# DFT odd sums added in the even sums' bank, with the low half and the doubled even sum taken out by ScalarE, and the patterns redrawn

## The chip, the cores and the metric

The kernel runs on one core of a Trainium2 chip. The metric is the device time of one execution in microseconds. The profile names the engines PE (TensorE, matmuls; PEld is its weight load), ACT (ScalarE), DVE (VectorE), POOL (GpSimd) and SP (SyncE, which only issues DMAs here). PE writes its results into eight banks of PSUM; ACT and DVE take them out from there.

## What is computed

```
X   = real(fft(fft(x, axis=1), axis=2))        # x: 8 x 3008 x 256, float32
h   = max(X.reshape(24064, 256) @ w_in, 0)     # w_in: 256 x 2048
out = (h * h) @ w_out                          # w_out: 2048 x 256
```

A Fourier transform over 3008 rows and 256 features, of which the real part is kept, and then a feed-forward layer with a squared ReLU.

## The kernel before

**Stage 1, the DFT over rows.** For each of the eight batches, DVE folds x into symmetric and antisymmetric parts (`fold_ops`, L353 to L390: operations on tiles u, v and w). PE multiplies w with cosine and sine tables (`cosT`, `sinT`). The sum over six row groups q is split into even and odd q (`par` 0 and 1), since the result at row k is even + odd and the result at the mirrored row is even - odd or odd - even. So two sums of some 377 columns give 754 columns of the tiles `pt` (cosine part, sn 0) and `qt` (sine part, sn 1). This is done for two blocks of columns (`blk` 0 and 1), so that each batch has four such pairs of sums; the batches in `INL`, 0 and 1, add six matmuls per `qt` pair for an extra row (`ez`), the others get that row from `e_ops`, for three batches at a time. `dft_ops` (L400) makes the list of pieces: a piece is three matmuls. In the kernel before, each sum has a PSUM bank of its own, the tile `pf`. When the even sum is complete ACT copies it to the tile `as` (L418); when the odd sum is complete DVE writes the low half (L453, or L449 with a sign) and the high half (L455, L457 or L450), each from `as` and the odd sum's bank. Batch 0's first block is done by `stage1_first` (L466).

**Stage 2, the first layer.** The feature transform is folded into w_in: `gmat` (L323) makes G1 and G2, `gneg` (L334) makes G3 = -2 G2 on all rows but the last. Columns of pt and qt go through in 25 chunks, two of 256 columns, then 512 each, the last of 264. A chunk that crosses the end of a batch has two segments, and each of its matmuls is split. A chunk has 16 units of 128 hidden features. A unit first makes G1 pt + G2 qt in a bank `xb`, takes out its ReLU, and then needs the same for the mirrored row. The kind of the unit, a letter in `KINDS`, says how the mirrored row is made:

- r: a third matmul with G3 into the same bank, and a second ReLU on ACT (L738)
- v: the third matmul too, and the ReLU on DVE (L735)
- d: no third matmul; DVE takes -2 xb + edge out between the two matmuls (L716), and adds it to xb afterwards (L727)
- q: as d, but ACT takes the first part out (L713) and POOL adds the edge (L714)
- p: as d, with the edge made by POOL (L694) and not by DVE (L697)

`x_front` and `x_take` start a unit, `x_back` ends it two steps later. `x_square` squares the results, two units at a time: on DVE (L750), or where `SQA` lists the pair on ACT in two halves (L747, L748).

**Stage 3, the second layer.** `mm2_ops` (L572): 128 matmuls of 256 columns for a full chunk into the tile `po`, copied by ACT (L618) to `os` and stored by SP.

**What sets the order.** Every engine runs its instructions in the order in which the program issues them, written out by hand: the loop at L886 goes through the units one step at a time and issues a front, half of the matmuls of an earlier chunk's second layer, a back, the other half, and then the deferred DVE writes (`DEFER`), the edges (`LEAD` steps ahead), the squares (`SQLAG` steps late) and whatever `spread` has put into `side` for this step: folds, DFT pieces, tables, loads. `FOLD` and `ST1` say over which share of a batch's steps they are spread. The six `xb`, `pf` and `pc` banks are handed round in turn, `po` has two.

**The head of the kernel.** SP loads x of batch 0, POOL gathers its mirrored rows in four parts (L99), POOL makes index tiles (`jrow`, L149), DVE and ACT make the tables, and SP loads w_in (L760) when ACT has finished the matrices `csD`, since `jrow` lies in the buffer of w_in. Then come loads of batch 1 (L136 and L112), and POOL's four loads of w_out into `wout16` (L766). `warm_up` issues matmuls on zeros. The stretch before the first unit is L770 to L812.

Of the kernel before, what the change touches and what calls it, by code (L numbers as in the profile page):

```python
# [10 lines left out]
F32 = mybir.dt.float32  # L11
# [3 lines left out]
ALU = mybir.AluOpType  # L15
# [9 lines left out]
def kernel(  # L25
# [116 lines left out]
    for s in range(2):  # L142
        nc.sync.dma_start(out=x4[0:NP, s, :, :], in_=up(0, s))
    load_mid(0, nc.sync)
    for q in (QH, 0):
        for s in range(2):
            gather_half(0, 1 - s, q)
    jrow = jm[:, 0]
    nc.gpsimd.iota(jrow, pattern=[[-1, P]], base=P - 1, channel_multiplier=0,  # L149
                   allow_small_or_imprecise_dtypes=True)  # L150
    idx = iota("idx", [P, 1], [[0, 1]], NP - 1, -1, I32)
    idx2 = iota("idx2", [P, 1], [[0, 1]], NQ // 2 * (NP - 1), -NQ // 2, I32)
    wout16 = const.tile([P, NFC, D], F16, name="wout16")
# [3 lines left out]
    def vec(name, w=1):  # L157
        return const.tile([P, w], F32, name=name)
# [20 lines left out]
    sgn = vec("sgn")  # L179
    s3 = vec("s3")  # L180
    nsgn = vec("nsgn")
    alt = vec("alt")
    alt2 = vec("alt2")
    nalt = vec("nalt")
# [10 lines left out]
    def sgn_vecs():  # L195
        nc.gpsimd.tensor_scalar(out=sgn, in0=pidx, scalar1=P - 1.5, scalar2=None, op0=ALU.is_lt)
        nc.gpsimd.tensor_scalar(out=s3, in0=sgn, scalar1=-2.0, scalar2=None, op0=ALU.mult)
        nc.gpsimd.tensor_scalar(out=sgn, in0=sgn, scalar1=2.0, scalar2=-1.0, op0=ALU.mult, op1=ALU.add)
        nc.gpsimd.tensor_scalar(out=nsgn, in0=sgn, scalar1=-1.0, scalar2=None, op0=ALU.mult)

    def absval(o, i):
        ts(out=o.bitcast(I32), in0=i.bitcast(I32), scalar1=0x7FFFFFFF, scalar2=None,
# [197 lines left out]
    def dft_ops(blk, mms, m, fin, run=3):  # L400
        c0, n = BLK[blk]
        st = {}
        ops = []

        def some(par, lo, hi):
            def f():
                ms = mms(par)
                if lo == 0:
                    st[par] = psx.tile([P, 512], F32, name="pf", tag="x")[:, 0:n]
                for i in range(lo, hi):  # L410
                    rows, wt, q, tab = ms[i]
                    mm(st[par][0:rows, :], wt(q), tab[k, q, c0 : c0 + n], i == 0,
                       i == len(ms) - 1)
                if hi < len(ms):
                    return
                if par == 0:
                    st["a"] = asp.tile([P, HE], F32, name="as", tag="as")[:, 0:n]
                    act(st["a"][0:m, :], st[0][0:m, :], AF.Copy, bias=0.0,  # L418
                        scale=1.0 if fin[0] is None else fin[0])
                else:  # L420
                    fin[1](st["a"][0:m, :], st[1][0:m, :])
            return f

        for par in range(2):
            nm = len(mms(par))
            ops += [some(par, i, min(i + run, nm)) for i in range(0, nm, run)]
        return ops

    def stage1_ops(b, blk, inline_e=False, run=3, later=None):
        later = (lambda f: f()) if later is None else later.append  # L430

        def lists(sn):
            def f(par):
                qs = range(par, NQ, 2)
# [7 lines left out]
            return f  # L442

        def fin(sn):
            def f(a, bp):
                hi = P - 1 if sn and not inline_e else P
                lo_, hi_ = halves(blk, PQ[b][sn][0:hi])
                if sn and inline_e:
                    stt(out=lo_, in0=a, scalar=sgn[:, 0:1], in1=bp, op0=ALU.mult, op1=ALU.add)  # L449
                    later(lambda: stt(out=hi_, in0=bp, scalar=nsgn[:, 0:1], in1=a, op0=ALU.mult,  # L450
                                      op1=ALU.add))
                else:
                    vt(lo_, a, bp, op=ALU.add)  # L453
                    if sn:
                        vt(hi_, a, bp, op=ALU.subtract)  # L455
                    else:
                        later(lambda: vt(hi_, bp, a, op=ALU.subtract))  # L457
            return f

        ops = []  # L460
        for sn in range(2):
            ops += dft_ops(blk, lists(sn), P - 1 if sn and not inline_e else P,
                           (sgn[:, 0:1] if sn and inline_e else None, fin(sn)), run)
        return ops

    def stage1_first(later):  # L466
        c0, n = BLK[0]
# [33 lines left out]
    def e_ops(bs):  # L501
        nb = len(bs)

        def start():
            t = esp.tile([4, NK], F16, name="es", tag="es")
            for i, b in enumerate(bs):
                est[b] = (t, i)

        def fin(blk):
            def f(a, bp):  # L510
                lo_, hi_ = halves(blk, est[bs[0]][0][0:nb])
                vt(lo_, a, bp, op=ALU.add)
                vt(hi_, bp, a, op=ALU.subtract)
            return f

        ops = [start]
        for blk in range(2):
            ops += dft_ops(blk, lambda par, blk=blk: [
                (MW, lambda q: ewide((blk * NQ + q) * B + bs[0]), q, cosT)
                for q in range(par, NQ, 2)], nb, (None, fin(blk)))  # L520
        return ops

    def e_row(b):
        t, i = est[b]
# [18 lines left out]
        g += n  # L543


    KINDS = ["vrvrrrvrrrrrrrrr"] + ["rvrrvrrrrrrrrrrr"] + ["rvrrvvrrrvrrrrrv"] + ["rrrrrrrrddqdrrrr"] + ["rdqqdrrdrrrvdrrd"] + ["rrrrddrrqrqdrqqd"] + ["rrrrrrqqqddrdrqd"] + ["rrdrqpqprdrrqrqr"] + ["drpddrqrpdqrdrdr"] + ["qddrqrdrrrddqdrr"] + ["drdqrdrqrrddrqdr"] + ["qrrddqqdvrdrqprr"] + ["prrdrpdrrddqdrqr"] + ["rqqdrdqrrqqrrddr"] + ["rrddqdqqrqqqrddq"] + ["rrrrrrqqqddqrqrq"] + ["dddrrdppqdpqdqrr"] + ["dpdrqdrqrqqdvqqr"] + ["qdqqdqrqrqdqqdrq"] + ["dqdrdqrddrqdrqpq"] + ["dpdqdqdrqrdprddr"] + ["qdqqdqrdqrqdrdqr"] + ["qdqddqrrdrqdrdqr"] + ["qdqqdqvrqrqdqrdp"] + ["rrppddpddddrppdd"]
    SQA = [(2,)] + [(1, 2)] + [(2, 6)] + [(1, 4, 5)] + [(0, 2, 3, 5, 6)] + [(0, 4, 6)] + [(1, 3, 7)] + [(1, 4, 6)] + [(0, 2, 5, 7)] + [(0, 2, 6, 7)] + [(3, 7)] + [(0, 2, 4, 6)] + [(0, 2, 5)] + [(2, 4, 6)] + [(2,)] + [(1, 4, 6, 7)] + [(1, 2, 4, 6)] + [(1, 4, 6)] * 2 + [(1, 4, 5, 6, 7)] + [(1, 4, 6)] * 3 + [(1, 4, 6, 7)] + [(0, 1, 2, 6)]

    LEAD = ["2222222222222222"] * 3 + ["2222222245222222"] + ["2322322822222222"] + ["2222462222222224"] + ["2222222262122228"] + ["2222248522222232"] + ["2262823222222222"] + ["2622222222222222"] + ["2272222222222262"] + ["4223722222225622"] + ["2222223222628222"] + ["2226222222222222"] + ["2224422722232222"] + ["2222222222222222"] + ["2222222226632222"] + ["2225222212222242"] + ["8223222222222222"] + ["2242322222482252"] + ["2222282222222222"] + ["2822222222282222"] + ["2222222222222222"] * 2 + ["2262232122422277"]
    DEFER = ["1111111111111111"] * 3 + ["1111111311131111"] + ["1101311111111111"] + ["1111221111111111"] + ["1111111111111111"] + ["1111113111111111"] + ["1112111111131111"] + ["1111112111121211"] + ["1101111111111111"] + ["1111211111111111"] + ["1111111111111111"] + ["1122111111111111"] + ["1111111111111111"] + ["1111111111111113"] + ["1111111111111111"] + ["1111101311111111"] + ["1111111111211111"] + ["1211101111011110"] + ["1111111111111111"] + ["1111111121131111"] + ["1111311211111111"] + ["1111111111131111"] + ["1101111101113111"]  # L550
    SQLAG = ["1112"] + ["3133"] + ["33323133"] + ["33333333"] + ["33333233"] + ["42331333"] + ["33331433"] + ["33333323"] + ["33344333"] + ["33323223"] + ["33333333"] + ["33333233"] * 2 + ["13333113"] + ["33333333"] * 2 + ["24333333"] + ["31333333"] + ["33233333"] + ["33333333"] * 2 + ["33233333"] + ["33333333"] * 2 + ["33334332"]

    gE = const.tile([P, NFC], F16, name="gE")
    gE2 = const.tile([P, NFC], F32, name="gE2")
# [145 lines left out]
    def x_take(c, u):  # L700
# [10 lines left out]
        X = edge(c, u)  # L711
        if KINDS[c][u] == "q":
            act(T, xb, AF.Copy, bias=0.0, scale=-2.0)  # L713
            nc.gpsimd.tensor_tensor(T, T, X, op=ALU.add)  # L714
        else:
            stt(out=T, in0=xb, scalar=-2.0, in1=X, op0=ALU.mult, op1=ALU.add)  # L716
        return (c, u, xb.unsqueeze(1), T)
# [77 lines left out]
        for _ in range(n):  # L795
            mm(warm, ez[:, 1, 0, :], ez[:, 1, 0:4, :], True, True)

    warm_up(6)
    gcast(0, nc.scalar.copy)
    hi_ops = []  # L800
    s1 = stage1_first(hi_ops)
    s1[0]()
    warm_up(2)
    gmat(0)
    s1[1]()
    s1[2]()
# [16 lines left out]
            side.setdefault(lo + int((hi - lo) * i / len(ops)), []).append(f)  # L823

    for c in range(1, F // 512):
        side.setdefault(c * (c - 1) // 2, []).extend([lambda c=c: gmat(c), lambda c=c: gneg(c)])

    spread(rd1[0:], 0, 5)
    spread(fo, 9, 10)
    spread(tr1[0:5], 12, 13)  # L830
    spread(tr1[5:], 11, 12)
    spread(mi1, 13, 14)
    spread(stage1_ops(0, 1, True), 14, 15)
    FOLD = {0: [(1, 0.475, 0.842)], 1: [(2, 0.02, 0.232), (3, 0.338, 0.664), (4, 0.6, 0.801)],
            2: [(5, 0.06, 0.96)], 3: [(6, 0.04, 0.96)], 4: [(7, 0.04, 0.85)]}
    ST1 = {0: (0.843, 0.905)}
    EGRP = {1: [2, 3, 4], 4: [5, 6, 7]}
    e_done = {}
    for b in range(B - 1):
# [126 lines left out]
```

## Time and profile before

| | us |
|---|---|
| four runs, median | 605.09 |
| lowest, highest | 604.77, 605.96 |
| the profiled execution | 604.93 |
| its span, first to last instruction | 603.0 |
| busy: PE, ACT, DVE, POOL | 581.4, 548.8, 523.8, 164.5 |
| first matmul of the second layer (po) | 37.67 |
| last matmul issued, last copy (L618) ends | 597.66 and on, 600.03 |

The page gives busy times of each engine, the span in 40 slices, and groups of instructions by line with their count, mean duration in ns, and the idle time of the engine before them with what ended it. Matmuls overlap in the pipeline, so their mean duration is longer than the distance from one to the next: 0.11 us for 256 columns, 0.16 for 376, 0.216 for 512 at full clock. Groups that the change touches: the copy of the even sum, L418, 31 of 505 ns and 3 signed ones of 576; the DVE halves, 544 to 547 ns, signed ones 606 to 610; the ACT square halves, 1059 and 1074; the DVE square, 1214 in the mean; POOL's add, 92 of 1292 in the mean.

### The profile page before, as it was taken

The page shows a single profiled execution, that of the slowest core. Times are in us where ns is not written, and L with a number is a line of the kernel's source. Part 1 is how long each engine was busy: PE and PEld are TensorE (multiplying, and loading weights), DVE is VectorE, ACT ScalarE, POOL GpSimd, SP SyncE. Part 2 cuts the span into 40 slices and gives each one's busy share as a digit, 9 for nine tenths or more (in the row PEclk, how much of TensorE's full clock was granted, in tenths as well). Part 3 has the DMA queues.
Part 4 walks back from the last instruction along what each step waited for, and adds up shares of the span by engine and source line. Part 5 has one row for each costly group of instructions (what it writes and reads, how often), then busy time and mean ns, then how long its engine had stood idle before and what let it go on. Part 6 is the DMA issues. An engine that isn't in the chain of part 4 may idle for free.

```text
span 603.0 us, 12237 instructions
## 1 busy us (share of the span) xinstructions
PE 581.4 (96%) x4543; PEld 437.3 (73%) x4543; DVE 523.8 (87%) x959; ACT 548.8 (91%) x963; POOL 164.5 (27%) x156
## 2 busy tenths in 40 slices
PE   2979999999999999999999999999999999999997
PEld 0647677777777777777777778777787778877786
DVE  7878898998898998898898997899889899999880
ACT  7888899999989999989998989999998999999981
POOL 5301022023322122312123043412443423324400
PEclk9979999999999999999999999999999999999999
DMA  7995484563483414913133115133242231332112
GB/s 238 276 111 144 119 229 154 172 242 49 64 255 49 62 41 69 244 49 45 55 61 45 52 39 60 45 45 58 58 63 41 50 53 54 45 61 56 55 54 71
DMA packets 41952, 56.24 MB, mean 93 GB/s; under 512 B 7746, under 2 KB 36726, under 8 KB 41894
## 3 DMA queue, kind: packets, MB, share of 16 engines
q1 hardware_dynamic: 37030, 42.04, 32.8%
q0 software_dynamic: 4864, 13.44, 8.5%
q8 instruction: 35, 0.57, 0.4%
q14 instruction: 23, 0.19, 0.1%
HBM read 29.02 MB, written 24.64 MB: 89 GB/s over the span
## 4 chain that ended last, share of the span: by engine, by line
PE 91%; DVE 4%; ACT 2%; POOL 1%; issue 1%; ACTq 0%; DVEq 0%; POOLq 0%
PE po L74 54%; PE xb L74 31%; PE pf L74 6%; POOL x L99 1%; DVE h L735 0%; DVE h L750 0%; ACT h L747 0%; ACT os L618 0%; ACT h L726 0%; DVE u L360 0%; DVE wst L212 0%; ACT bs L713 0%; DVE v L369 0%; DVE w L373 0%; DVE tm L268 0%
## 5 line engine op out<-in xcount | busy, mean ns | idle before, releaser
L74 PE MATMUL po<-wout,h 128*128 128x256 f16 x3024 | 451.6, 273 | 4.2 <-DVE h L735 3.6
L74 PEld LDWEIGHTS <-h 128*128 128x128 f16 x3024 | 286.7, 98 | 114.5 <-issue 5.5
L74 PE MATMUL xb<-qt,G 128*128 128x512 f16 (+10 forms) x743 | 208.0, 322 | 1.2 <-ACT h L671 0.8
L714 POOL TENSOR_TENSOR bs<-bs,h 128x512 f32<-128x512 f32 x92 | 118.6, 1292 | 316.0 <-ACT bs L713 256.7
L727 DVE CUSTOM_DVE_ANT_0 h<-xb,bs 128x512 f16<-128x512 f32 (+1 forms) x231 | 144.6, 638 | 22.9 <-ACT h L726 22.0
L74 PE MATMUL xb<-pt,G 128*128 128x512 f16 (+16 forms) x512 | 146.7, 324 | 1.0 <-DVE h L727 0.4
L726 ACT ACTIVATE h<-xb 128x512 f16<-128x512 f32 (+1 forms) x218 | 135.4, 623 | 7.8 <-PE xb L74 5.5
L74 PEld LDWEIGHTS <-G 128*128 128x128 f16 x1255 | 120.6, 98 | 24.3 <-issue 2.8
L750 DVE TENSOR_TENSOR h<-h 128x2048 f16<-128x2048 f16 (+1 forms) x113 | 137.0, 1214 | 0.8 <-ACT h L738 0.7
L671 ACT ACTIVATE h<-xb 128x512 f16<-128x512 f32 (+1 forms) x166 | 103.8, 629 | 9.3 <-PE xb L74 8.4
L738 ACT ACTIVATE h<-xb 128x512 f16<-128x512 f32 (+2 forms) x155 | 95.8, 621 | 11.2 <-PE xb L74 9.5
L716 DVE SCALAR_TENSOR_TENSOR bs<-xb,h 128x512 f32<-128x512 f32 (+1 forms) x126 | 82.9, 659 | 18.5 <-PE xb L74 15.2
L748 ACT ACTIVATE h<-h 128x1024 f16<-128x1024 f16 (+1 forms) x79 | 84.9, 1074 | 0.0
L747 ACT ACTIVATE h<-h 128x1024 f16<-128x1024 f16 (+1 forms) x79 | 83.7, 1059 | 0.1
L697 DVE TENSOR_SCALAR h<-eb,gE 128x512 f16<-128x512 f16 (+1 forms) x198 | 69.9, 368 | 0.1
L618 ACT ACTIVATE os<-po 128x512 f32<-128x512 f32 (+1 forms) x95 | 59.5, 627 | 8.9 <-PE po L74 8.9
L713 ACT ACTIVATE bs<-xb 128x512 f32<-128x512 f32 x92 | 57.3, 623 | 3.2 <-PE xb L74 2.0
L112 POOL DMA_INDIRECT x<-in_x_dram,idx x16 | 21.0, 1314 | 79.2 <-DVE u L364 62.4
L360 DVE TENSOR_TENSOR u<-x 127x765 f16<-127x765 f32 x32 | 29.5, 947 | 0.0
L74 PEld LDWEIGHTS <-w 127*128 127x128 f16 (+1 forms) x192 | 22.1, 119 | 8.6 <-DVE w L373 3.1
L74 PE MATMUL pf<-cosT,w 127*128 127x377 f16 (+1 forms) x96 | 20.6, 329 | 2.2 <-DVE w L373 2.2
L373 DVE TENSOR_TENSOR w<-v 127x384 f16<-127x384 f16 x64 | 22.1, 369 | 0.0
(111 smaller groups left out, 211.3 us busy)
## 6 DMA issues: line engine op xcount, KB each, us to landing
out_dram<-os SPq DMA_DIRECT2D x157, 128.0 KB
x<-in_x_dram SPq DMA_DIRECT2D x16, 756.0 KB
wst<-in_moe_w_in_dram SPq DMA_DIRECT2D x4, 512.0 KB
eb<-qt SPq DMA_DIRECT2D x14, 128.0 KB
wout<-in_moe_w_out_dram POOLq DMA_DIRECT2D x4, 256.0 KB, 18.8
x<-in_x_dram,idx POOLq DMA_INDIRECT x20, 9.8
gE<-G SPq DMA_DIRECT2D x16, 0.2 KB
x<-in_x_dram SPq DMA_DIRECT2D x14, 2.0 KB
```

Of the source, the lines that this page charges most:

```text
L74: nc.tensor.matmul(o, l, r, start=start, stop=stop, skip_group_check=True)
L618: act(os_[:, js], po[:, js], AF.Copy, bias=0.0, scale=HS * HS)
L671: act(r_s(c, u), xb, AF.Relu, scale=-1.0)
L697: ts(out=X, in0=ebc[c][:, 0:n], scalar1=gE2[:, u : u + 1], scalar2=None, op0=ALU.mult)
L714: nc.gpsimd.tensor_tensor(T, T, X, op=ALU.add)
L716: stt(out=T, in0=xb, scalar=-2.0, in1=X, op0=ALU.mult, op1=ALU.add)
L726: act(r_s(c, u), xb, AF.Relu, scale=-1.0)
L727: mirrors.append((int(DEFER[c][u]), lambda: relu_d(c, u, lambda o, i: nc.vector._custom_dve(TENSOR_ADD_SAT, out=o[:, 0, :], in0=xb[:, 0, i ...
L738: relu_d(c, u, lambda o, i: act(o, xb[:, :, i], AF.Relu, scale=-1.0))
L747: act(h2[:, 0:nf], h2[:, 0:nf], AF.Square)
L748: rest.append(lambda: act(h2[:, nf:], h2[:, nf:], AF.Square))
L750: vt(h2, h2, h2, op=ALU.mult)
```

## The change

The odd matmuls go on adding in the bank of the even sum. Between the two, ACT copies the even sum, doubled (with a sign vector `sgn2` where a sign is needed). When all matmuls are through, the bank holds even + odd, the low half: ACT copies it out, and DVE makes the high half from the bank and the doubled even sum. So each pair of sums takes one bank and one DVE operation, and two ACT operations. `stage1_first` stays as it was. The pieces of `e_ops` now run as even, even, odd, odd over the two blocks. POOL's add of a q unit is cut into two halves. In the head, the iota of `jrow` stands after the second gather instead of after the fourth; ten warm-up matmuls stand ahead of the first DFT sums and none behind them (six and two before); the ACT copy `gcast(0)` is issued after them. The second and third `gmat` stay at their steps. Some `spread` ranges of the head move, and batch 1's DFT pieces are spread over a larger stretch.

The pattern strings are drawn anew. In all: r 168 to 158, v 14 to 18, d 106 to 108, q 92 to 95, p 20 to 21; pairs squared on ACT 79 to 72; entries of `LEAD` other than 2 from 56 to 88, of `DEFER` other than 1 from 32 to 41.

```diff
@@ the head
-    for q in (QH, 0):
-        for s in range(2):
-            gather_half(0, 1 - s, q)
     jrow = jm[:, 0]
-    nc.gpsimd.iota(jrow, pattern=[[-1, P]], base=P - 1, channel_multiplier=0,
-                   allow_small_or_imprecise_dtypes=True)
+    for i in range(4):
+        gather_half(0, 1 - i % 2, (QH, 0)[i // 2])
+        if i == 1:
+            nc.gpsimd.iota(jrow, pattern=[[-1, P]], base=P - 1, channel_multiplier=0,
+                           allow_small_or_imprecise_dtypes=True)
@@ sgn_vecs
+        nc.gpsimd.tensor_scalar(out=sgn2, in0=sgn, scalar1=2.0, scalar2=None, op0=ALU.mult)
@@ dft_ops
-                if lo == 0:
-                    st[par] = psx.tile([P, 512], F32, name="pf", tag="x")[:, 0:n]
+                if lo == 0 and par == 0:
+                    st[0] = psx.tile([P, 512], F32, name="pf", tag="x")[:, 0:n]
                 for i in range(lo, hi):
                     rows, wt, q, tab = ms[i]
-                    mm(st[par][0:rows, :], wt(q), tab[k, q, c0 : c0 + n], i == 0,
+                    mm(st[0][0:rows, :], wt(q), tab[k, q, c0 : c0 + n], par == 0 and i == 0,
                        i == len(ms) - 1)
...
                     act(st["a"][0:m, :], st[0][0:m, :], AF.Copy, bias=0.0,
-                        scale=1.0 if fin[0] is None else fin[0])
+                        scale=2.0 if fin[0] is None else fin[0])
                 else:
-                    fin[1](st["a"][0:m, :], st[1][0:m, :])
+                    fin[1](st["a"][0:m, :], st[0][0:m, :])
@@ stage1_ops
-            def f(a, bp):
+            def f(a2, lo):
                 hi = P - 1 if sn and not inline_e else P
                 lo_, hi_ = halves(blk, PQ[b][sn][0:hi])
+                act(lo_, lo, AF.Copy, bias=0.0, scale=1.0)
                 if sn and inline_e:
-                    stt(out=lo_, in0=a, scalar=sgn[:, 0:1], in1=bp, op0=ALU.mult, op1=ALU.add)
-                    later(lambda: stt(out=hi_, in0=bp, scalar=nsgn[:, 0:1], in1=a, op0=ALU.mult,
-                                      op1=ALU.add))
+                    stt(out=hi_, in0=lo, scalar=nsgn[:, 0:1], in1=a2, op0=ALU.mult, op1=ALU.add)
+                elif sn:
+                    vt(hi_, a2, lo, op=ALU.subtract)
                 else:
-                    vt(lo_, a, bp, op=ALU.add)
-                    if sn:
-                        vt(hi_, a, bp, op=ALU.subtract)
-                    else:
-                        later(lambda: vt(hi_, bp, a, op=ALU.subtract))
+                    vt(hi_, lo, a2, op=ALU.subtract)
@@ e_ops
-                vt(lo_, a, bp, op=ALU.add)
-                vt(hi_, bp, a, op=ALU.subtract)
+                act(lo_, lo, AF.Copy, bias=0.0, scale=1.0)
+                vt(hi_, lo, a2, op=ALU.subtract)
...
-        return ops
+        return [start] + [o[i] for i in range(2) for o in ops]
@@ x_take
-            nc.gpsimd.tensor_tensor(T, T, X, op=ALU.add)
+            for i in range(0, n, CH // 2):
+                w = slice(i, i + CH // 2)
+                nc.gpsimd.tensor_tensor(T[:, w], T[:, w], X[:, w], op=ALU.add)
@@ the start of the units
-    warm_up(6)
-    gcast(0, nc.scalar.copy)
+    warm_up(10)
     hi_ops = []
     s1 = stage1_first(hi_ops)
     s1[0]()
-    warm_up(2)
+    warm_up(0)
+    gcast(0, nc.scalar.copy)
     gmat(0)
...
-    spread(fo, 9, 10)
+    spread(fo, 12, 13)
     spread(tr1[0:5], 12, 13)
-    spread(tr1[5:], 11, 12)
+    spread(tr1[5:], 12, 13)
...
-    ST1 = {0: (0.843, 0.905)}
+    ST1 = {0: (0.9, 0.99)}
```

## The prediction

> **What bounds the kernel now.** I read the page's engine and clock rows first, then a table by stage, then PE's list of waits, and last the timeline around PE's one long gap. All durations are from one profiled execution: 604.93 us, of which the span is 603.0 and 1.93 lies around it. The median of the four runs shown is 605.09 us, 0.16 above; the sum below starts from 604.93.
>
> ```profile
> PE 581.4 (96%) x4543; PEld 437.3 (73%) x4543; DVE 523.8 (87%) x959; ACT 548.8 (91%) x963; POOL 164.5 (27%) x156
> ...
> PEclk9979999999999999999999999999999999999999
> ```
> PE is nearly always busy, and the granted clock falls once, in the third slice. By stage (columns: busy time of PE, PEld, DVE, ACT, POOL, then granted clock, DMA share, GB/s):
>
> ```profile
> 32.00:35.42 3.42, 1.31 (x10) 0.73 (x8) 3.39 (x6) 3.42 (x7) 0.00 (x0) 1.00 1.52 191
> 35.42:42.25 6.83, 4.58 (x22) 3.19 (x22) 4.91 (x16) 5.01 (x12) 0.00 (x0) 0.50 0.87 95
> ...
> 45.00:570.00 525.00, 524.36 (x4125) 394.03 (x4124) 472.14 (x824) 493.50 (x851) 148.66 (x123) 1.00 0.39 85
> ```
> From 45 to 570 us PE idles for 0.64 of 525 us, while ACT idles for 31.5 and DVE for 52.9. PE's waits after 45 us are three:
>
> ```profile
> PE po L74 <- ACT os L618: 0.5, 1, 0.5
> PE xb L74 <- DVE h L727: 0.4, 1, 0.4
> PE xb L74 <- ACT h L671: 0.2, 1, 0.2
> ```
> The first is at 597 us, in the tail. So from 42 us on the time is the sum of PE's instructions: a saving on DVE or ACT is worth nothing by itself, and any wait given to PE costs its full length. Before that, PE stands still once:
>
> ```profile
> 33.76 0.10 PEld L74 LDWEIGHTS <-h 128*128 128x128 f16 x1
> ...
> 37.67 1.01 PE L74 MATMUL po<-wout,h 128*128 128x256 f16 x4 [3.63 <-DVE h L735]
> ```
> The page blames a DVE write, but the weight h is already loaded at 33.76; what is missing is the other operand, wout. Its first DMA is issued at 19.41, and the tile's landings read
>
> ```profile
> DMA to landing us min/median/max: 18.2/18.8/19.9
> ```
> 19.41 + 18.2 = 37.61, and the matmul starts at 37.67. The head is bound by DMA, and after the gap PE runs at half clock until 42.25: 4.58 us at half rate, 2.29 lost.
>
> **The change, part by part.** Counts are from the instruction order of the two programs.
>
> *(1) Fewer matmuls.* A unit of kind r or v needs a third matmul (G3) that d, q and p do not. r falls from 168 to 158, v rises from 14 to 18; d, q, p gain 2, 3, 1. All six units that lose the third matmul lie in one-segment chunks (10, 11, 13 twice, 14, 16), so six matmuls of 512 columns go. Two such matmuls start at 21.86 (pc) and the next at 22.29: 0.43 for two, 0.216 each. 6 x 0.216 = **-1.3 us**, all on PE.
>
> *(2) One bank instead of two for the DFT sums.* The odd matmuls now write the bank that ACT is copying, so they wait for that copy. In batches 2 to 7 the halves stand about 2.8 steps apart, 3 to 5 us by the pf rows of before (97.54, 100.64, 105.48), and the copy ends at most 2.8 us after its sums (97.86 to 100.56): no wait. The row-group sums (es) are reordered so that another block stands between the halves: no wait. In batch 0's second block and in batch 1 the halves follow each other directly in PE's order at five of six places; at the sixth seven matmuls, about 1.1 us, stand between. The same spot in before:
>
> ```profile
> 44.03 1.12 PE L74 MATMUL pf<-cosT,w 127*128 127x376 f16 x6
> 44.71 0.48 ACT L418 ACTIVATE as<-pf 128x376 f32<-128x376 f32 x1
> 44.99 0.64 PE L74 MATMUL pf<-cosT,ez 127*128 127x376 f16 x3
> ...
> 46.15 0.57 ACT L418 ACTIVATE as<-pf,sgn 128x376 f32<-128x376 f32 x1 [0.95 <-PE pf L74]
> ```
> Six matmuls take 44.99 - 44.03 = 0.96, so the first three are through at 44.51; the copy ends at 45.19 and PE could go on at 45.24 (0.05 is the step from an ACT end, 32.90, to the matmul it frees, 32.95). Wait: 0.73. The signed copy follows sums that are through at 45.95 and ends at 46.72: 0.82. Two places of the first kind (0.73), two of the second (0.82), and one where an output copy (L618, 0.63) stands ahead on ACT, 0.9: **+4.0 us**. Queued behind the waiting matmul is all of PE. Ends: 0, if PE would wait there anyway, and 7, if ACT is as late as at 62.16, where the sums were through and the copy ended at 63.63 (1.5 x 5). I take the nearest row, 4.0.
>
> *(3) Work between ACT and DVE.* DVE loses 34 low-half sums (27 x 0.55 + 3 x 0.61 + 4 x 0.54 = 18.8 us); ACT gains 34 copies of 0.49 to 0.58, about 16.9. Seven square pairs move from ACT (2.13 each, -14.9) to DVE (1.21 each, +8.5). The kinds move ACT by -4.4 (r -12.5, v +2.5, d +1.2, q +3.7, p +0.6) and DVE by +10.3 (v 2.7, d 3.3, q 3.0, p 1.3). Sums: ACT -2.4, DVE 0.0, of 549 and 524: nothing, and PE covers both. If that cover fails, a DVE high half that waits for ACT's low copy holds all of DVE; the queue on ACT ahead of a copy is 0 to 2.2 us by the rows above, at 28 places. Those waits fall first into the 21 idle stretches, 12.1 us, that DVE already spends there waiting for PE's pf. Bounds for PE: -0.6 (two late waits vanish with the redrawn patterns) to +3. I take -0.3.
>
> *(4) POOL's adds in halves.* 92 adds of 1.29 become 190 of half width. Between 0.58 (half of 1.16, their median) and 1.16 each; POOL idles 316 us ahead of them, so even the dear end (+100 us) is largely covered. A DVE operation that met two adds took 1.26 instead of 0.34 (449.66, POOL busy 448.50 to 450.77); halves may shorten this. 0 for PE, inside the bounds of (3).
>
> *(5) The head.* The iota for jrow moves ahead of the last two gathers (they start 0.3 later). DVE waited 1.70 us for it at 8.03; now L212 can start at 6.33, the matrices end sooner, and SP, which sat 7.9 us on csD, issues the w_in loads about 1.9 us earlier. That does not shorten the DMA work; it fills a lull: from 11.9 to 13.6 us the loads move at 149 GB/s, against some 300 before, 1.7 x 0.5 = 0.85 us. So wout lands near 36.8; ends 36.0 and 37.9 (loads that slow the gathers). The gain is partly spent: before the first po matmul PE now has six 256-column matmuls (0.11 each) fewer behind it, +0.65. And if the clock rises at 42.25 again, 0.85 us more at half rate yields only 0.42. -0.42 + 0.65 = **+0.2**; bounds -1.8 (clock back one 3.41 us step earlier) to +1.5. The ten warm-ups, against six and two, end before or with the first pf matmul at 14.1 and cost nothing, being covered by the wait for w and then for wout.
>
> Sum: 604.93 - 1.3 + 4.0 - 0.3 + 0.2 = **607.5 us**.
>
> [...]
>
> **Rivals.**
> *A, faster: the five waits are hidden.* PE would be waiting there anyway, for squares or late wout quarters, so that the copies run in idle time. For it: ACT and DVE are busy for 30.2 and 31.3 of the 35 us from 45 to 80. Against it: PE idles nowhere between 42.25 and 80. It decides if another wait of over 0.8 us stands at each place: 607.5 - 4.0 = 603.5. Chance 0.10.
> *B, about equal: the head gives more.* The clock is back a step earlier (-1.7) and wout is at 36.8 or before: 607.5 - 1.7 = 605.8 or a little less. For it: the step's position against the kernel's start may vary. Chance 0.22.
> *C, slower still: DVE waits for ACT's low copies and passes it on* as late squares to PE; from where DVE's 52.9 us of slack is locally used up. +2 to +3: about 610. Chance 0.13.
> That the change does not do what it says is no rival: the counts are in the program.
>
> **How the numbers follow.** Forecast 607.5, own range 606.2 to 608.9: 0.55. A measurement can tell about 0.2% from no change, so faster is below 603.9 and slower above 606.3. Faster: A and a little of B, 0.14. Within: the rest of B and the low edge, 0.26. Slower: 0.60. The range reaches into A's upper edge and C: 604.2 to 609.8.
>
> **What would show it.** Right: gaps on PE of 0.7 to 0.9 us at five pf matmuls between 42 and 70 us, released by the copy; 332 G2/G3 matmuls of 512 columns against 338; no pf gap after 95 us; first po near 36.8. Wrong: PE dense between 42 and 70 (A); the half-clock stretch one step long (B); PE waits on DVE over 2 us after 80 us (C).

## The result, and the profile after

The changed kernel takes **605.94 us** in the median of 49 runs (604.76 to 607.96), the kernel before 604.84 us in 76 runs on the same chips (602.93 to 607.72). The ratio is 1.0021, with a 95% interval of 1.0015 to 1.0026: slower, by 1.1 us in the medians. The profiled execution took 605.47 us (span 603.6), 0.54 above the profiled one of before. So the direction was forecast rightly, but 605.94 lies just under the forecast's own range (606.2 to 608.9): over half of the forecast move of 2.6 us (607.5 against 604.93) is missing.

The page of the changed kernel, its PE and clock rows:

```profile
PE 579.6 (96%) x4539; PEld 436.2 (72%) x4539; DVE 523.3 (87%) x950; ACT 544.6 (90%) x976; POOL 187.5 (31%) x256
...
PEclk9979999999999999999999999999999999999999
```

PE has four records fewer: six third matmuls of 512 columns are gone, and two warm-up matmuls were added. DVE is where it was, ACT 4 us lower, and PE remains the engine that sets the time.

By stage (columns as in the prediction: busy PE, PEld, DVE, ACT, POOL, granted clock, DMA share, GB/s):

```profile
32.00:35.42 3.42, 0.00 (x0) 0.00 (x0) 2.80 (x3) 2.58 (x5) 0.00 (x0) 0.66 1.47 162
35.42:42.25 6.83, 6.74 (x42) 5.09 (x42) 2.75 (x7) 3.44 (x8) 0.00 (x0) 0.67 0.42 40
...
45.00:570.00 525.00, 522.41 (x4107) 392.25 (x4106) 471.25 (x815) 489.85 (x862) 170.55 (x221) 1.00 0.39 85
```

Two things have moved. In the first two rows PE's idle stretch is over before 35.6 and not at 37.67, and the half-clock stretch lies earlier too: it runs from 33.1 to 39.9, again 6.83 us long, so that each of the two windows shows a mixed clock (0.66, 0.67). In the last row PE idles for 2.59 us, where it idled for 0.64. What it waits for after 42 us stands in PE's list of waits (us in total, times, longest):

```profile
PE pf L74 <- ACT as L420: 3.2, 5, 0.7
PE po L74 <- ACT os L616: 0.5, 1, 0.5
```

Five waits for the copy of the even sum (L420, the L418 of before), and the tail's old wait. The timeline of PE shows where the first of them are, and the new start of the second layer:

```profile
35.52 1.01 PE L74 MATMUL po<-wout,h 128*128 128x256 f16 x4 [4.39 <-DMA wout<-in_moe_w_out_dram]
...
43.38 0.65 PE L74 MATMUL pf<-cosT,w 127*128 127x376 f16 x3
44.75 0.64 PE L74 MATMUL pf<-cosT,w 127*128 127x376 f16 x3 [0.71 <-ACT as L420]
45.22 0.64 PE L74 MATMUL pf<-cosT,ez 127*128 127x376 f16 x3
45.70 0.64 PE L74 MATMUL pf<-sinT,w 127*127 127x376 f16 x3
47.07 0.64 PE L74 MATMUL pf<-cosT,ez 127*128 127x376 f16 x3 [0.72 <-ACT as L420]
```

Pieces of three matmuls follow each other at 0.47 to 0.48 us; the piece at 44.75 comes 1.37 after its predecessor and the one at 47.07 likewise, 1.37 after 45.70. The bracket counts only the time in which no matmul was in flight, so it says 0.71 and 0.72. What PE loses is the excess of the distance from start to start: 0.88, 0.89, 0.74, 0.73 and 0.83, at the matmuls that start at 44.75, 47.07, 64.22, 68.93 and 72.28 us. That is 4.06 us in sum (from unrounded times).

DVE's list of waits after 42 us holds something that the kernel before did not have:

```profile
DVE pt L454 <- ACT pt L448: 6.6, 8, 2.2
DVE qt L450 <- ACT qt L448: 5.0, 3, 3.3
DVE qt L452 <- ACT qt L448: 4.9, 6, 1.8
DVE es L511 <- ACT es L510: 1.6, 2, 0.8
```

In 19 places DVE stands still, 18.1 us in sum, until ACT has copied the low half out. No line of this kind appears in PE's list, so here it costs next to nothing (from start to start, 0.3 us at two places).

### The profile page after: what moved, and what is told of

It reads as the page before. It is cut to its first block, busy times and chain, and to the rows that moved or that the text cites. A ratio compares the mean times of both kernels' runs of the same rounds, so it can differ in the third digit from the quotient of the medians.

```text
span 603.6 us, 12339 instructions
## 1 busy us (share of the span) xinstructions
PE 579.6 (96%) x4539; PEld 436.2 (72%) x4539; DVE 523.3 (87%) x950; ACT 544.6 (90%) x976; POOL 187.5 (31%) x256
## 4 chain that ended last, share of the span: by engine, by line
PE 91%; DMA 4%; ACT 2%; POOL 1%; issue 1%; DVE 0%; POOLq 0%; ACTq 0%
PE po L74 54%; PE xb L74 31%; PE pf L74 6%; DMA wout<-in_moe_w_out_dram 3%; DMA x<-in_x_dram,idx 1%; POOL x L99 0%; ACT as L420 0%; POOL x L112 0%; ACT os L616 0%; ACT cosT L285 0%; ACT h L669 0%; ACT sinT L289 0%; ACT h L726 0%; ACT h L747 0%; DVE qt L452 0%
## 5 line engine op out<-in xcount | busy, mean ns | idle before, releaser
L714 POOL TENSOR_TENSOR bs<-bs,h 128x256 f32<-128x256 f32 x190 | 141.0, 764 | 289.3 <-ACT bs L711 227.4
L74 PE MATMUL xb<-qt,G 128*128 128x512 f16 (+10 forms) x737 | 205.2, 322 | 0.4 <-DVE qt L487 0.3
L727 DVE CUSTOM_DVE_ANT_0 h<-xb,bs 128x512 f16<-128x512 f32 (+1 forms) x237 | 148.0, 638 | 19.5 <-ACT h L726 14.9
L750 DVE TENSOR_TENSOR h<-h 128x2048 f16<-128x2048 f16 (+1 forms) x120 | 144.6, 1209 | 0.2
L716 DVE SCALAR_TENSOR_TENSOR bs<-xb,h 128x512 f32<-128x512 f32 (+1 forms) x129 | 84.8, 659 | 17.7 <-PE xb L74 14.0
L738 ACT ACTIVATE h<-xb 128x512 f16<-128x512 f32 (+2 forms) x145 | 89.8, 621 | 6.7 <-PE xb L74 5.2
L748 ACT ACTIVATE h<-h 128x1024 f16<-128x1024 f16 (+1 forms) x72 | 77.5, 1076 | 0.0
L747 ACT ACTIVATE h<-h 128x1024 f16<-128x1024 f16 (+1 forms) x72 | 76.3, 1059 | 0.1
L616 ACT ACTIVATE os<-po 128x512 f32<-128x512 f32 (+1 forms) x95 | 59.6, 628 | 8.9 <-PE po L74 8.9
L711 ACT ACTIVATE bs<-xb 128x512 f32<-128x512 f32 x95 | 59.6, 628 | 2.0 <-DVE h L727 1.0
L112 POOL DMA_INDIRECT x<-in_x_dram,idx x16 | 18.2, 1138 | 81.3 <-DVE u L366 64.2
```

The costliest lines, as they stand in the source:

```text
L74: nc.tensor.matmul(o, l, r, start=start, stop=stop, skip_group_check=True)
L616: act(os_[:, js], po[:, js], AF.Copy, bias=0.0, scale=HS * HS)
L714: nc.gpsimd.tensor_tensor(T[:, w], T[:, w], X[:, w], op=ALU.add)
L727: mirrors.append((int(DEFER[c][u]), lambda: relu_d(c, u, lambda o, i: nc.vector._custom_dve(TENSOR_ADD_SAT, out=o[:, 0, :], in0=xb[:, 0, i ...
L738: relu_d(c, u, lambda o, i: act(o, xb[:, :, i], AF.Relu, scale=-1.0))
L747: act(h2[:, 0:nf], h2[:, 0:nf], AF.Square)
```

## The experiments

After the result the theory was this. After the first po matmul PE sets the time, and the five round trips to ACT cost their 4 us, as priced. The head gave more than forecast (by 1.9 us, if the two profiles are compared), and it gave it through the iota: w_in's loads are issued earlier, and so the DMA work ends earlier and wout lands earlier. The rivals: the missing time comes from the work shifted between ACT, DVE and POOL; or from the clock, or from the warm-up matmuls. Each ratio is against the kernel before on the same chip; differences in us between two of the other kernels are between medians, often from different chips.

### The five waits: the DFT pieces woven

```diff
-        return ops[0] + ops[1]
+        return ops[0][: h[0]] + ops[1][: h[1]] + ops[0][h[0] :] + ops[1][h[1] :] if inline_e else ops[0] + ops[1]
```

In the changed kernel, for the batches in `INL`, the even sums of pt and qt come first and the odd ones after them, so that another sum stands between the two halves of one bank.

> The changed kernel with the DFT pieces of batch 0's second block and of batch 1 in another order: the even sums of pt and qt first, then their odd sums, so that other matmuls stand between an even sum and its odd sum. If the five waits of 4.06 us in all are a plain loss on PE, at most one short wait of some 0.3 us a block stays, and the time falls by 3 to 4 us below the changed kernel's, to about 602. If PE would stand still there anyway (later for the values, or for a bank), the waits return at the next units, and the time falls by less than 1.

Measured: 602.39 us, ratio 0.9954 [0.9938, 0.9970], 3.55 us below the changed kernel. Of the five waits two are left, each of 0.2 in the list of PE's waits (0.41 and 0.35 from start to start):

```profile
PE po L74 <- DMA wout<-in_moe_w_out_dram: 4.3, 2, 3.8
PE po L74 <- ACT os L616: 0.5, 1, 0.5
PE pf L74 <- ACT as L420: 0.4, 2, 0.2
```

4.06 - 0.76 = 3.30 us of waits went, and 3.55 us of time. Where six other matmuls (0.95 us) stand between the two halves of a bank, the shared bank cost nothing here; where three stand there (0.47 us), up to 0.4 us was left.

### The new DFT undone, and the new DFT alone

`bank_back` is the changed kernel with the DFT of before: a bank for each sum, and both halves on DVE (the hunks `dft_ops`, `stage1_ops` and `e_ops` of the diff undone). `bank_alone` is the kernel before with these hunks alone; patterns and head stay as they were.

> The changed kernel with the DFT as before (a bank for each sum, both halves by VectorE), under the new patterns and the new head. The five waits of 4.06 us go, VectorE takes back 18.8 us of work and ScalarE loses 16.9. If the five waits are the whole price of the bank change, the time is 601.5 to 602.5, as with the woven pieces. If the new patterns, drawn for a VectorE relieved of this work, now overload it, waits of PE on VectorE come up after 80 us and the time is above 604.

> The kernel before with the shared bank alone (the DFT pieces, the copies on ScalarE and the order of the row-group sums); patterns, head and POOL's adds as before. Six direct places where the odd sum follows its even sum: batch 0's second block 2, batch 1 up to 4, each 0.73 to 0.9, so +4.0 to +5 us by the sum on record, some 609 to 610, if the patterns have no part in it. If the old patterns load ScalarE too much (it gains 16.9 us of work), further waits of PE on ScalarE and VectorE appear after 80 us and it is 611 or more.

Measured: `bank_back` 602.94 us, 0.9968 [0.9955, 0.9980], 3.0 below the changed kernel. Its list of PE's waits from 25 us on:

```profile
PE po L74 <- DMA wout<-in_moe_w_out_dram: 5.0, 1, 5.0
PE po L74 <- ACT os L620: 0.5, 1, 0.5
PE xb L74 <- ACT h L742: 0.3, 1, 0.3
PE xb L74 <- DVE qt L451: 0.2, 1, 0.2
PE xb L74 <- ACT h L673: 0.2, 1, 0.2
```

There are no waits for `as`, and DVE, which carries 14.7 us more (538.0 against 523.3), passes next to none of it on: its largest line there is 0.2 us. `bank_alone` took 617.0 us, 1.0195 [1.0178, 1.0212], 12 us above before. Its list of PE's waits from 25 us on:

```profile
PE pf L74 <- ACT as L420: 4.8, 6, 1.4
...
PE xb L74 <- DVE qt L452: 2.2, 3, 1.3
PE xb L74 <- DVE h L725: 1.5, 4, 0.5
PE xb L74 <- ACT h L736: 0.8, 3, 0.3
PE xb L74 <- ACT h L669: 0.6, 1, 0.6
PE xb L74 <- DVE pt L454: 0.5, 1, 0.5
```

From start to start the six `as` waits cost 5.8 us, and fifteen waits for DVE and ACT after 80 us cost 7.5, of which the kernel before has 1.1 itself: 5.8 + 7.5 - 1.1 = 12.2, and 12.0 are measured. ACT is busy for 560.4 us there (548.8 before) and DVE for 508.6 (523.8 before): DVE, which gained time, is the one that hands over late most often. Its own list of waits from 42 us on says why:

```profile
DVE pt L454 <- ACT pt L448: 19.2, 13, 2.5
...
DVE qt L452 <- ACT qt L448: 13.0, 9, 3.0
DVE qt L450 <- ACT qt L448: 6.6, 3, 2.2
DVE es L511 <- ACT es L510: 4.9, 3, 3.1
```

At 28 of the 34 places where a low copy goes ahead of a high half, DVE waits for it, 43.7 us in sum (19 places and 18.1 us in the changed kernel). That is rival C's mechanism, and with the old patterns it is real. In the changed kernel PE no longer meets it. What brings it down is, by elimination, the redrawn patterns (or the larger stretch for batch 1's pieces): the head acts before 45 us, and POOL's halves do nothing to the time (below). Which part of the patterns does it was not run.

### The head: the iota put back, and the iota moved alone

`iota_back`, in the changed kernel:

```diff
-        if i == 1:
+        if i == 3:
```

`iota_alone` is the kernel before with the changed kernel's loop over the gathers, and nothing else.

> The changed kernel with the iota of jrow put back behind the fourth gather; nothing else is undone. If the iota brings the head's gain (w_in loads issued 1.8 us earlier, wout landing at 35.47 in place of 37.62), the first w_in load is issued near 12.0 again, wout lands at 37.3 to 37.7, the first po matmul starts there, and the time is 1.5 to 2.2 us above the changed kernel's, some 607.2 to 608. If the gain comes from the warm-ups and the moved cast, or is only how the DMAs happened to run in the one profiled execution, wout still lands near 35.5 and the time stays within 0.5 us of the changed kernel's.

> The kernel before with the iota of jrow moved between the second and third gather; nothing else. If the iota alone moves the chain of loads, wout lands near 35.5 and the time falls by 1.5 to 2.2 us, to about 603. If the other changes of the head are needed for it, wout stays near 37.6 and the time near 604.9.

Measured: `iota_back` 606.96 us, 1.0031 [1.0020, 1.0042], 1.0 above the changed kernel in the medians and 0.6 by the two ratios, whose intervals overlap (1.5 to 2.2 was expected); w_in's loads are issued at 11.97 again (10.13 in the changed kernel). `iota_alone` 602.94 us, 0.9963 [0.9948, 0.9978], 2.1 below the kernel before on its chip, clear of noise. The first po matmul in the timelines of PE, of `iota_back` and of `iota_alone`:

```profile
36.94 1.01 PE L74 MATMUL po<-wout,h 128*128 128x256 f16 x4 [5.50 <-DMA wout<-in_moe_w_out_dram]
```

```profile
35.62 0.60 PE L74 MATMUL po<-wout,h 128*128 128x256 f16 x4 [1.04 <-DMA wout<-in_moe_w_out_dram]
```

In the second the four matmuls take 0.60 and not 1.01 us: PE had idled for 1.04 us only, and the clock stayed at full rate, so this execution gains twice. Only three of the twelve runs list a clock of 1.000, so the median has the first gain and seldom the second. The first landings of wout in all profiles that keep the order of the loads tell what the iota does:

| iota behind the fourth gather | wout lands | iota behind the second | wout lands |
|---|---|---|---|
| before | 37.62 | iota_alone | 35.58 |
| bank_alone | 37.03 | after | 35.47 |
| iota_back | 36.90 | woven | 35.32 |
| before_keep | 36.32 | bank_back | 35.98 |
| | | warm_back | 35.82 |
| | | pool_whole | 35.25 |
| | | woven_warm | 36.20 |
| mean | 36.97 | mean | 35.66 |

The gain is 1.3 us in the means, between 0.85 (forecast) and 2.15 (the two profiles first compared): the profiled execution of before was the latest of its group by 0.6. The groups do not overlap, but nearly touch (36.32 and 36.20), and each entry is one execution.

### Warm-ups and POOL's halves

`warm_back`: the changed kernel with six and two warm-up matmuls and `gcast(0)` ahead of the DFT sums, as before. `pool_whole`: the changed kernel with one POOL add per q unit.

```diff
-    warm_up(10)
+    warm_up(6)
+    gcast(0, nc.scalar.copy)
...
-    warm_up(0)
-    gcast(0, nc.scalar.copy)
+    warm_up(2)
```

```diff
-            for i in range(0, n, CH // 2):
-                w = slice(i, i + CH // 2)
-                nc.gpsimd.tensor_tensor(T[:, w], T[:, w], X[:, w], op=ALU.add)
+            nc.gpsimd.tensor_tensor(T, T, X, op=ALU.add)
```

> The changed kernel with the warm-up matmuls and the first cast as before (six ahead, the cast, two behind). If the ten warm-ups only bring PE's early work forward and so lengthen its wait for wout (4.4 us against 1.0 with the iota alone), the first unit starts 1 to 1.7 us later, near 21, the wait is 1 us shorter or more, wout lands where it did, and the time is equal or up to 1.5 us shorter, shorter if the clock then holds in some runs. If the early clock is worth its time, the kernel is 0.5 to 1.5 us slower than the changed one.

> The changed kernel with GpSimd's adds in one piece as before (95 of 128x512 in place of 190 halves). By the sum on record the halves cost and bring PE nothing: 605.9, within 0.6 us. If they keep VectorE's operations from being held by a whole add, PE waits for VectorE appear late in the kernel and the time is 1 us or more above the changed kernel's.

Measured: 605.80 us, 1.0021 [1.0009, 1.0034], and 605.68 us, 1.0016 [1.0004, 1.0028]. Both are 0.1 to 0.3 us from the changed kernel, inside the intervals: neither part does anything to the time that can be seen. The first xb matmul is at 19.44 in `warm_back` and at 19.78 in the changed kernel, so the ten warm-ups did not bring the first unit forward either, as had been thought (near 21 was expected). POOL's groups, of the changed kernel and of `pool_whole` (busy us and mean ns behind the bar):

```profile
L714 POOL TENSOR_TENSOR bs<-bs,h 128x256 f32<-128x256 f32 x190 | 141.0, 764 | 289.3 <-ACT bs L711 227.4
```

```profile
L712 POOL TENSOR_TENSOR bs<-bs,h 128x512 f32<-128x512 f32 x95 | 122.6, 1294 | 306.9 <-ACT bs L711 238.2 <-DVE h L695 46.5 <-DVE bs L714 11.6
```

Two halves take 1.53 us where one whole takes 1.29. POOL idles for about 300 us ahead of them either way.

### The clock held up by dummy matmuls

Sixteen matmuls of 512 columns (`csD` times G1) into the bank of po, ahead of the first po matmul, in the kernel before (`before_keep`) and in the woven one (`woven_warm`). The sums that follow overwrite what they write.

```diff
+                    if c == 0 and grp is groups[0]:
+                        for _ in range(16):
+                            mm(st["o"].rearrange("p j d -> p (j d)"), csD[:, 0, 0, :], G1[:, 0:512],
+                               True, True)
```

> The kernel before with 16 matmuls of 512 columns on values that nobody reads ahead of the first po matmul, in the bank that it overwrites; nothing is left out. They fill 3.5 of the 3.63 us of PE's wait for wout. If the half-clock stretch costs 2.29 us here as in the sum on record, the clock stays at 1.0 and the time falls by 1.5 to 2.5 us, to about 603. If the clock falls in only some of the runs of before, by less.

> The woven kernel with 16 matmuls of 512 columns on values that nobody reads, put ahead of the first po matmul, into the bank that this one then overwrites; nothing is left out. At full clock they take 3.5 us, inside the 4.2 us in which PE waits for wout. If the half-clock stretch after the wait follows from PE's idleness in it, the clock stays at 1.0 and the time falls by some 1 to 2.2 us below the woven kernel's, and its runs lie closer together. If the clock falls anyway, or the dummies delay the first po, the time is equal or up to 1 us longer.

Measured: `before_keep` 603.79 us, 0.9984 [0.9969, 0.9998], 0.7 below before on its chip; `woven_warm` 601.62 us, 0.9945 [0.9932, 0.9957], 0.8 below `woven`. The clock does stay up (the runs list 0.997 to 1.000, and neither profile has a half-rate stretch around the first po), but only 0.7 and 0.8 us come of it, less than expected, and the second is within the noise. Part of the reason is in the runs of before: not each of them has 6.83 us at half rate. On that chip six list a clock of 0.994 (median 604.6) and six 0.997 (603.6), so that difference is worth about 1 us there, and many executions had only about half of the loss (the profile of before, with 6.83 us at half rate, lists 0.994; 3.41 us at half rate would make 0.997 of 603 us, as an estimate, and `woven` lists that). What eats the rest (runs of `before_keep` at 1.000 took 603.9, no less than those of before at 0.997) was not taken apart.

### w_out's loads first

In three kernels POOL issues the four loads of w_out ahead of the loads of batch 1 and not behind them: `woven_wout` (on `woven`), `bank_wout` (on `bank_back`) and `iota_wout` (on `iota_alone`).

```diff
-    for f in rd1[0:0] + fe[1][0:3] + [lambda: load_x(1)] + fe[1][3:]:
+    for f in rd1[0:0] + fe[1][0:3] + [load_w_out, lambda: load_x(1)] + fe[1][3:]:
...
-    load_w_out()
```

> The woven kernel with the four loads of w_out issued ahead of the gathers of batch 1 on GpSimd's queue, which puts them near 11 us in place of 19 to 20. If the head is bound by the DMAs ahead of wout, wout lands long before PE comes to it (near 31), the wait of some 4 us goes, the half-clock stretch may go with it, and the time falls by 3 to 6 us to 597 to 599. If w_in, which now shares the queues, is delayed by more than that, or the head is bound by ScalarE and VectorE just behind wout, the gain is under 2 us.

> The changed kernel with the DFT as before, a bank for each sum, and the loads of w_out ahead of batch 1's gathers. With separate banks there is no wait for a copy at all, against two of 0.35 us in the woven form, and VectorE carries 18.8 us more. If VectorE's work is covered, 597 to 598; if not, 599 or more.

> The kernel before, old bank and old patterns, with two edits of the head: the iota of jrow between the second and third gather, and the loads of w_out issued ahead of batch 1's gathers. If the new patterns are worth only their 1.3 us of matmuls, this comes to 598 to 599.5, about 1 us above the woven kernel with the same load order (597.6). If the old patterns hold VectorE or ScalarE back once wout is there early, 600 or more.

Measured:

| kernel | median, us | ratio [95% interval] | first po |
|---|---|---|---|
| woven_wout | 597.61 | 0.9878 [0.9862, 0.9893] | 31.47 |
| bank_wout | 597.64 | 0.9889 [0.9868, 0.9911] | 30.59 |
| iota_wout | 599.82 | 0.9924 [0.9902, 0.9945] | 32.67 |

PE's timeline of `woven_wout` at the start of the second layer:

```profile
31.47 0.60 PE L74 MATMUL po<-wout,h 128*128 128x256 f16 x4
32.24 0.38 PE L74 MATMUL xb<-qt,G 128*128 128x256 f16 x2 [0.17 <-ACT h L669]
33.76 0.61 PE L74 MATMUL po<-wout,h 128*128 128x256 f16 x4 [1.14 <-DVE h L750]
```

The gap (3.85, 5.04 and 1.04 us in the kernels that these are built on) is gone, in all three profiles the first po matmul waits for nothing, and with the gap the half clock goes: 14 of the 16 runs list 1.000. In `woven_wout` the loads are issued at 11.59 to 13.96, and not from 20.0 on as in `woven`. The gathers of batch 1 pay for it (they land at 37.33 and 40.28, in the changed kernel at 30.21 and 34.55), and nothing on PE waits for them. `woven_wout` and `bank_wout` are the best versions of the study, 7.2 us below before and 8.3 below the changed kernel. The DFT in one bank, woven, and the DFT in two banks end level: 597.61 and 597.64. `iota_wout`, with the old patterns, lies 2.2 above them and not 1; its first po matmul comes 1.2 and 2.1 later, with 72 xb matmuls ahead of it where the others have 66.

## Why the prediction was right in part and wrong in size

Set against the medians, the terms read so:

| term | forecast | measured | from |
|---|---|---|---|
| (1) six matmuls fewer | -1.3 | counted, not run alone | PE x4539: -6 and 2 more warm-ups |
| (2) five waits for `as` | +4.0 | +4.06 | start to start; `woven` -3.55, `bank_back` -3.0 |
| (3) late waits for DVE, ACT | -0.3 | -0.55 | 1.13 us of them in before, 0.58 in after |
| (4) POOL halves | 0 | 0 | `pool_whole` 0.26 lower, inside the interval |
| (5) the head | +0.2 | -1.1 | what is left of +1.1 in the medians, with -1.3 for (1) |

Term (1) is the one that no run shows by itself: `bank_back` and `iota_alone`, which differ by the patterns and the rest of the head, both take 602.94 us.

**What bounds the kernel** was right. PE sets the time after the first po matmul, and the wait for wout, not the DVE write that the page of before blamed, ends the gap ahead of it: the loads of wout issued earlier take the gap away.

**Step (2)** was right to 0.1 us, in number, place and size, although read from a kernel that has no such wait: the spacing of six matmuls, the end of a copy on ACT, and 0.05 for the step between them were enough. Even the dearer place came as said: at 43.72 an output copy (L616, 0.60 us) stands ahead of the first copy of an even sum. The five waits, 0.73 to 0.89 us each, follow from the program, since the odd matmuls add onto the very values that the copy reads. But their cost is not fixed: with the order of the sums in `woven`, 3.30 of the 4.06 us went.

**Step (3)** had the right sign. It names 28 places at which DVE could be held by ACT's low copies; the program has 34, and DVE is held at 19, for 18.1 us. They reach PE only with the old patterns (`bank_alone`), so the cover that this step relied on goes with the redrawn patterns, and does not need the DVE time saved: in `bank_back` DVE has that work back and PE loses nothing by it.

**Step (5) failed: the gain of the earlier landing was sized far too low.** The step put it at 0.85 us, from the lull between 11.9 and 13.6, and then halved it, since the clock would rise at 42.25 again. Both were wrong. The means of the table give 1.3 for the landing, and the pair of profiles 2.15. And the clock does not come back at a fixed time of the kernel: it is back at 39.92 us in the changed kernel and at 42.25 in before. After the first po matmul PE spends 4.4 us at half rate in the changed kernel and 4.6 in before, so the gain in landing came through whole.

The other part of the step was right. It added 0.65 us for six xb matmuls that now stand behind the first po. In the profiles 66 xb matmuls stand ahead of it, and 72 in before. From its start to the end of the span the changed kernel takes 568.1 us and before 565.3, 2.8 more; -1.3 + 0.65 + 4.06 - 0.55, and 0.1 less for the clock, make 2.8. So in the medians the earlier landing has to be worth 1.1 + 0.65 = 1.75 us, where the step had 0.42.

The iota is shown to move the landing and the time in the kernel before (`iota_alone`, -2.1 us). In the changed kernel putting it back costs 0.6 to 1.0 us, with an uncertainty of about 0.7. Whether the iota accounts for all of the 1.75 there stays open; the warm-ups and the moved cast do not (`warm_back`).

The lull is filled, as the step said. The row by stage of before and of the changed kernel (last column GB/s):

```profile
12.00:16.00 4.00, 1.76 (x6) 0.81 (x6) 3.86 (x9) 3.67 (x10) 0.00 (x0) 1.00 0.75 209
```

```profile
12.00:16.00 4.00, 2.90 (x14) 1.30 (x13) 3.65 (x9) 1.87 (x7) 0.00 (x0) 1.00 0.99 315
```

106 GB/s more for 4 us are 0.42 MB. As an estimate, they take 1.2 to 1.7 us at the 248 to 347 GB/s that before moves in the 8 us that follow. The step had counted only the lowest 1.7 us of a low stretch of four.

**The rivals.** A did not happen: PE idles at each of the five places. B's number (605.8) was hit, but by luck: the head gave more through wout, and not through a clock that is back one step of 3.41 us earlier against the first po (4.4 us after it, and 4.6 in before). No row of before or of the changed kernel shows the step that B and the bounds of (5) use by itself: 3.41 is half of the 6.83 us that both profiles have at half rate, and the listed clocks show executions with about half of that loss (0.997 against 0.994). C did not happen with these patterns, and is real with the old ones.

## What to carry to other kernels

A PSUM bank shared by two halves cost a round trip to the engine that reads it (0.73 to 0.89 us, for a copy of 376 columns) at the five places of the changed kernel where the second half follows at once in PE's order, and nothing in `woven` where 0.95 us of other matmuls stands between; so change the order before giving up the bank. Busy time saved on an engine that does not set the time was worth nothing by itself: moving the low halves from DVE to ACT brought nothing with one set of patterns (`woven` and `bank_back` are level, 602.39 and 602.94 us) and went with some 6 us of late waits on PE under the other. Where PE stands still once in the head, look for the operand that is missing and not for the releaser on the page, and issue its load ahead of what is needed later: that was worth 3.1 to 5.3 us here (`iota_alone` to `iota_wout`, `bank_back` to `bank_wout`), where the whole change moved 1.1.

## What the runs showed of the hardware

- The half-clock stretch around the first po starts 1.4 us after PE has gone idle ahead of it in before (at 35.42 us) and 2.0 us after in the changed kernel (at 33.10), and is 6.83 us long in both. In `woven` PE goes idle at 31.51, the four po matmuls at 35.36 still take 0.60 us, and the four at 36.66 take 1.01; its profile lists a clock of 0.997, which makes some 3.6 us at half rate (0.003 of 600.2 us, doubled; an estimate). The eight profiles with a gap of 2.8 to 5.5 us ahead of the first po matmul have po matmuls at half rate (1.01 us for four) at its end, `woven` 1.3 us later; in those with 1.0 and 1.4 us (`iota_alone`, `woven_warm`) the four take 0.60 and the profile lists 1.000.
- The nine runs of `iota_alone` that list a clock of 0.994 to 0.997 took about 603.2 us, the three at 1.000 took 601.1: near such a gap a kernel has executions 2 us apart, and one profile of it is not its median.
- Two halves of POOL's add took 0.23 us more than one whole (2 x 764 ns in the changed kernel, 1294 in `pool_whole`): an add of 256 columns took 59% of one of 512.
- The 1024 packets of 2 KB that bring w_in took 90 ns in the mean in the changed kernel and 105 in before, with the same median of 84 and longer stragglers in before (up to 759 ns, against 380). Why they straggled stays open: it is one profile of each.
